# A transformer block's training step on one core: probability gradients, K heads and Q heads of the backward segments in two head halves

## The chip, the cores and the metric

The kernel runs on one core of one Trainium2 chip. The metric is the time of the whole program on the device, in microseconds (us), as a median over runs. All runs quoted here are in the same (fast) state.

Short names: PE is the tensor engine, DVE the vector engine, ACT the scalar engine, POOL GpSimd. L1129 is line 1129 of the kernel in question; the change moves lines, so that the same work has other numbers in the changed kernel (a table follows below).

## The reference, cut to what matters

A residual block: layer norm, attention with a recurrent memory of 8 rows, layer norm, SwiGLU feed-forward; then the gradients for all inputs and weights. The sequence of 2048 tokens is worked in 64 segments of 32 tokens, each with the 8 memory rows ahead of it (L = 40), 16 heads of width 256, model width 448.

```python
for s in range(n_seg):                                   # 64 segments, one after the other
    h = jnp.concatenate([mem, xs], axis=1)               # 8 memory rows + 32 tokens
    q, k, v = (einsum('btd,dhe->bhte', h, W) for W in (Wq, Wk, Wv))
    p = softmax(where(mask, einsum('bhqe,bhke->bhqk', q, k) * scale, -1e9))
    o = einsum('bhte,hed->btd', einsum('bhqk,bhke->bhqe', p, v), Wo)
    mem = o[:, :M, :]                                    # feeds the next segment
    outs.append(o[:, M:, :])
...
_out, _vjp = jax.vjp(_f, A_x, A_mem0, A_Wq, A_Wk, A_Wv, A_Wo, B_w_gate, B_w_up, B_w_down)
_grads = _vjp(grad_out)
```

The recurrence goes backwards in the gradient: the backward part walks the 64 segments from last to first, and each needs the gradient of the memory rows from the one before it. This serial walk is what the change is about.

## The kernel before

The program has four stages, one after the other: 64 forward segments, the feed-forward part, 64 backward segments, and a tail with the weight gradients. Here is one backward segment, in the kernel's order. `k.ps1()` takes a PSUM bank from a pool of five, `k.fx1()` one from a pool of two, and `k.evac` copies a bank out with DVE ("v") or ACT ("s").

```python
for s in range(NSEG - 1, -1, -1):
    t, r = divmod(s, 4)                       # r: place in the tile of 4 segments, 3 comes first
    ...
    pss = [k.ps1() for _ in range(4)]
    ...  matmul(pss[..], WoT_sb, do_roll)     # L1152 output gradients, 128 of them
    ...  evac(doT, pss[b])
    token_major(0); token_major(1)            # L1161 turned output gradients, copied by DVE / ACT
    pD = k.ps1()
    ...  matmul(pD, doT, vT)                  # L1170 probability gradients, 32
    ...  four DVE instructions pD -> dS_bd    # L1177-L1182 score gradients, all 8 head pairs at once
    heads("v", dO_sb, P_bd)                   # L1129, 16 matmuls into three banks, then copies
    rows_in("v", WvT_sb, 0, MC)               # L1201 row products, MC = 32
    heads("k", Q_sb, dS_bd)                   # L1129: needs dS_bd
    ...  turned scores, 16 small matmuls      # L1210
    rows_in("k", WkT_sb, 0, 20)
    heads("q", K_sb, dST_bd)                  # L1129: needs the turned scores
    rows_in("k", WkT_sb, 20, MC)
    rows_in("q", WqT_sb, 0, MC)
    ...
    pm = k.ps1()
    ...  matmul(pm, om, sel)                  # L1223 closing fp32 products
    ...  vector.tensor_copy(do_roll[next], pm3[:, :, 24:32])          # what the next segment needs
    nc.scalar.copy(out=dxT[:, :, r * SEG + M:(r + 1) * SEG], in_=pm3[:, :, 0:24])   # L1234
    if r == 0:                                # once per 4 segments: the block of memory rows
        px = k.fx1()
        ...  96 row products into px          # L1265: fill gaps of the NEXT segments on PE
        pl = k.fx1()
        ...  4 fp32 products into pl          # L1272 (8 instructions in the trace for the 4)
        pX = k.fx1()
        ...  4 fp32 transposes of dxT         # L1280: read the whole of dxT
        ...  layer-norm backward, store
```

First, PE works in different *forms*: the whole array (128x128), half (64 columns wide), or four strips of 32 columns; the row products run four at once, one per strip, and such a group of four is called a slot: in the trace the four start 3 to 4 ns apart, each lasts 353 ns (median), and one slot starts 0.189 us after another. Second, a scheduler orders the instructions by priority, so the 96 row products of the block of memory rows (L1265) slide into gaps of the following segments, and the fp32 work behind them (L1272, L1280) follows once they are complete.

## Time and profile before

| | us |
|---|---|
| time, median of 3 runs | 3078.84 (3069.54 to 3079.16) |
| forward stage and what lies between it and the next (profiled run) | 1030.9 |
| feed-forward stage | 301.6 |
| 64 backward segments | 1028.7 |
| tail | 713.6 |
| PE busy, whole program | 2910.6 (94%) |

The stages are read from the start times of PE's instructions in the trace: from the first query and key product of the first forward segment (L536), from the first feed-forward product (L891), from the first L1152, from the last segment's L1152 to the end. The profiled run was 3091.27.

The 64 backward segments come in four kinds, by `r`. Their periods, from one segment's first L1152 to the next one's (medians), are 16.07 us for r = 3 (15.91 in the undisturbed ones), 15.91 for r = 2, 16.79 for r = 1, 15.87 for r = 0. I call r = 3 and r = 2 the usual segments.

### The profile page before, as it was taken

How to read it: one execution, taken by the hardware profiler on the slowest of the kernel's cores; microseconds unless marked ns; L12 is line 12 of the kernel's file. 1: busy time of each engine (PE TensorE's matmuls, PEld its weight loads, DVE VectorE, ACT ScalarE, POOL GpSimd, SP SyncE). 2: the span in 40 equal slices, each digit the busy share in tenths (PEclk: the TensorE clock that was granted, in tenths of full speed). 3: DMA queues.
4: the chain of work that ended last, by engine and by line, in shares of the span. 5: the costliest groups of instructions: out<-in, count | busy, mean ns of one | idle time of the engine just before them, and what ended most of it. 6: DMA issues, size and time to landing. Idle time of an engine off the chain costs nothing.

```text
span 3089.5 us, 108321 instructions
## 1 busy us (share of the span) xinstructions
PE 2910.6 (94%) x47650; PEld 1739.2 (56%) x47650; DVE 1366.9 (44%) x3445; ACT 1054.3 (34%) x2570; POOL 676.0 (22%) x1507
## 2 busy tenths in 40 slices
PE   5999999999998999989999999999999899999999
PEld 3455555555554555556776677667776444444444
DVE  4555555555555576654545555455555001111110
ACT  2444444444444444433333333333333011111120
POOL 2222222222222222321212122212212111212111
PEclk9999999999999999989999999999999999999999
DMA  7567766766767989984455545545455998969971
GB/s 243 136 169 179 184 166 174 187 169 175 190 178 184 278 218 220 218 287 125 135 150 137 140 131 139 155 131 145 133 134 169 273 270 216 183 183 190 176 200 52
DMA packets 739468, 550.12 MB, mean 178 GB/s; under 512 B 600052, under 2 KB 635364, under 8 KB 736564
## 3 DMA queue, kind: packets, MB, share of 16 engines
q1 hardware_dynamic: 687956, 389.65, 53.0%
q0 software_dynamic: 51040, 153.54, 15.2%
q8 instruction: 374, 6.13, 0.8%
q14 instruction: 98, 0.80, 0.1%
HBM read 168.01 MB, written 234.23 MB: 130 GB/s over the span
## 4 chain that ended last, share of the span: by engine, by line
PE 68%; issue 11%; DMA 7%; DVE 7%; ACT 4%; POOL 2%; SPq 1%; ACTq 0%; POOLq 0%; DVEq 0%
PE po L1201 7%; PE psf L1152 7%; PE psf L536 6%; PE psf L653 5%; PE po L698 4%; PE psf L1376 4%; PE psf L1129 3%; PE psf L891 3%; PE fx L1015 3%; PE fx L1265 3%; PE psf L1223 2%; PE fx L465 2%; DVE arA L75 2%; PE psf L1398 2%; PE psf L550 2%
## 5 line engine op out<-in xcount | busy, mean ns | idle before, releaser
L75 DVE CAST arA<-psf 128x256 bf16<-128x256 f32 (+3 forms) x933 | 425.4, 478 | 786.2 <-PE psf L1376 275.5
L76 ACT CAST arA<-psf 128x96 bf16<-128x96 f32 (+4 forms) x915 | 353.5, 409 | 1030.7 <-PE psf L1376 261.2
L1201 PE MATMUL po<-arW,arA 128*32 128x448 bf16 x6144 | 348.1, 356 | 7.6 <-DMA arW<-Tq 3.7
L1376 PE MATMUL psf<-arW,arA 128*128 128x512 bf16 x980 | 250.2, 383 | 0.0
L1376 PEld LDWEIGHTS <-arA 128*128 128x128 bf16 x1440 | 137.1, 99 | 167.4 <-issue 19.0
L1201 PEld LDWEIGHTS <-arA 128*32 128x32 bf16 x6144 | 158.6, 97 | 126.3 <-DVE arA L75 8.4
L1152 PEld LDWEIGHTS <-arW 128*128 128x128 bf16 x8192 | 213.3, 96 | 24.3 <-issue 24.3
L1152 PE MATMUL psf<-arA,arW 128*128 128x40 bf16 x8192 | 216.7, 179 | 5.7 <-DVE arA L1227 5.1
L653 PE MATMUL psf<-arW,arA 128*64 128x512 bf16 x1536 | 216.5, 382 | 0.0
L536 PE MATMUL psf<-arW,arA 128*32 128x512 bf16 x3072 | 193.8, 385 | 12.5 <-DVE arA L739 12.5
L76 ACT COPY arA<-psf 128x512 bf16<-128x512 bf16 (+3 forms) x206 | 149.2, 725 | 120.9 <-DVE arA L75 77.3
L76 ACT CAST arB<-psf 128x64 bf16<-128x64 f32 (+3 forms) x384 | 121.9, 318 | 157.8 <-PE psf L540 106.6
L698 PE MATMUL po<-arW,arA 128*32 128x256 bf16 (+1 forms) x4096 | 141.1, 263 | 10.3 <-DVE arA L75 7.7
L75 DVE COPY arA<-psf 128x512 bf16<-128x512 bf16 (+2 forms) x204 | 104.2, 511 | 101.7 <-PE psf L550 55.8
L891 PE MATMUL psf<-arW 128*128 128x256 bf16 (+1 forms) x1288 | 146.4, 274 | 2.7 <-DVE arA L75 1.3
L891 PEld LDWEIGHTS <-arW 128*128 128x128 bf16 (+1 forms) x1344 | 102.3, 97 | 53.0 <-issue 42.1
L536 PEld LDWEIGHTS <-arA 128*32 128x32 bf16 x3072 | 70.5, 96 | 90.0 <-DVE arA L739 18.1
L1129 PEld LDWEIGHTS <-arW 128*128 128x128 bf16 x2048 | 84.4, 99 | 62.5 <-issue 53.9
L465 PE MATMUL fx<-arA,arW 128*128 128x64 bf16 (+1 forms) x2048 | 84.4, 195 | 32.6 <-ACT arB L76 19.0
L1398 PE MATMUL psf<-arW 128*128 128x448 bf16 x525 | 111.1, 352 | 0.8 <-DMA arW<-X_o 0.8
L698 PEld LDWEIGHTS <-arA 128*32 128x32 bf16 x4096 | 93.5, 96 | 32.4 <-DVE arA L75 10.9
L1438 POOL DMA_DIRECT2D out_dram<-arA x96 | 52.0, 549 | 264.3 <-DVE arA L75 260.0
(285 smaller groups left out, 4562.5 us busy)
## 6 DMA issues: line engine op xcount, KB each, us to landing
arW<-T SPq DMA_DIRECT2D x256, 128.0 KB
X_o<-arA SPq DMA_DIRECT2D x37, 512.0 KB
T<-arA SPq DMA_DIRECT2D x64, 256.0 KB
X_v<-arA POOLq DMA_DIRECT2D x32, 512.0 KB, 4.7
X_k<-arA POOLq DMA_DIRECT2D x32, 512.0 KB, 3.9
X_q<-arA POOLq DMA_DIRECT2D x32, 512.0 KB, 3.8
out_dram<-arA POOLq DMA_DIRECT2D x90, 128.0 KB, 4.3
VG<-arA SPq DMA_DIRECT2D x64, 160.0 KB
```

What stands on the lines that cost most here:

```text
L75: return nc.vector.tensor_copy(out=out, in_=in_)
L76: return nc.scalar.copy(out=out, in_=in_)
L465: nc.tensor.matmul(banks[w][:, i * 64:(i + 1) * 64], lhsT=lhsT, rhs=xr[lo:hi, kc, :], start=(kc == 0 and i == 0), stop=(kc == KC - 1), ski ...
L536: nc.tensor.matmul(banks[w][32 * q:32 * q + 32, :], lhsT=hT_roll[:, kc, sl, M:L], rhs=(Wq_sb, Wk_sb)[w][:, kc, col(q, b)], start=(kc == 0) ...
L653: nc.tensor.matmul(pV[b][64 * g:64 * g + 64, 0:512], lhsT=hT_flat[:, kc, sl * L:sl * L + 64], rhs=Wv_sb[:, kc, n * 512:(n + 1) * 512], sta ...
L698: nc.tensor.matmul(pO[32 * q:32 * q + 32, 0:w], lhsT=xblk[:, j, r * SEG:(r + 1) * SEG], rhs=Wo_sb[:, cj(j), 256 * dh:256 * dh + w], start= ...
L891: nc.tensor.matmul(ps[fp][:, f2 * 256:(f2 + 1) * 256], lhsT=Wt[lo:hi, kc, c * P:(c + 1) * P], rhs=xT[lo:hi, kc, :], start=(kc == 0 and f2 ...
L1129: nc.tensor.matmul(ps[b][:, i * 2 * L:(i + 1) * 2 * L], lhsT=lhs[:, at, :], rhs=rhs_bd[:, cl // 2, :, :].rearrange("p g n -> p (g n)"), st ...
L1152: nc.tensor.matmul(pss[b][:, jj * L:(jj + 1) * L], lhsT=WoT_sb[:, kc, c * P:(c + 1) * P], rhs=do_roll[:, kc, sl, :], start=(kc == 0), stop ...
L1201: nc.tensor.matmul(pH[32 * (j % 4):32 * (j % 4) + 32, 0:D], lhsT=blk[nm][:, j, r * SEG:(r + 1) * SEG], rhs=WT[:, cj(j), :], start=(nm == " ...
L1376: nc.tensor.matmul(pa[2 * kc + g][:, 0:w], lhsT=lhs_of(b)[:, kc * P:(kc + 1) * P], rhs=rhs_of(b, g), start=(b == 0), stop=(b == nblk - 1), ...
L1398: k.last_mm = nc.tensor.matmul(pa[i][:, 0:D], lhsT=lhs_of(b, i), rhs=rhs_of(b), start=(bi == 0), stop=(bi == m + 3))
```

## The change

The intent: K heads wait for the score gradients of all heads. If probability gradients, score gradients, K heads, turned scores and Q heads go in two halves of the heads, the first half can be under way on DVE while PE does something else, and no engine waits for the other. In the forward part, the values of heads 0 to 3 move ahead of the rest of V; in the feed-forward part, the down product takes its bank from the pool of five.

```diff
@@ forward segment
             value_rows(3)
+            values(0)
             value_rest(2, p_in)
...
-            values(0)
@@ feed-forward
-            pf = k.fx1()
+            pf = k.ps1()
@@ backward segment (cut)
-            for h in range(8):
-                ...                                  # probability gradients of all heads
-            ...                                      # score gradients, 4 DVE instructions
+            def grad_of_probs(b):
+                for h in range(4 * b, 4 * b + 4): ...
+            def grad_of_scores(b): ...               # the same 4 DVE instructions on half of the columns
+            for b in range(2):
+                grad_of_probs(b)
+                grad_of_scores(b)
...
             heads("v", dO_sb, P_bd)
-            rows_in("v", WvT_sb, 0, MC)
-            heads("k", Q_sb, dS_bd)
-            ...                                      # turned scores, all
-            rows_in("k", WkT_sb, 0, 20)
-            heads("q", K_sb, dST_bd)
-            rows_in("k", WkT_sb, 20, MC)
+            rows_in("v", WvT_sb, 0, 20)
+            half_heads("k", Q_sb, dS_bd, 0)
+            turned_scores(0)
+            rows_in("v", WvT_sb, 20, MC)
+            half_heads("k", Q_sb, dS_bd, 1)
+            turned_scores(1)
+            half_heads("q", K_sb, dST_bd, 0)
+            rows_in("k", WkT_sb, 0, 12)
+            half_heads("q", K_sb, dST_bd, 1)
+            rows_in("k", WkT_sb, 12, MC)
             rows_in("q", WqT_sb, 0, MC)
```

The line numbers of the same work:

| work | before | after |
|---|---|---|
| probability gradients | L1170 | L1173 |
| score gradients (DVE) | L1177 to L1182 | L1180 to L1185 |
| V heads | L1129 | L1129 |
| K and Q heads | L1129 | L1215 |
| row products | L1201 | L1232 |
| turned scores | L1210 | L1241 |
| closing fp32 products | L1223 | L1261 |
| ACT copy of `pm` to `dxT` | L1234 | L1272 |
| memory rows: row products, fp32 products, fp32 transposes | L1265, L1272, L1280 | L1303, L1310, L1318 |

More of the change, by code (lines that the diff above doesn't have):

```diff
@@ L1165, in backward_chain, with grad_of_scores @@
             pD = k.ps1()
-            for h in range(8):
-                for g in range(2):
-                    for dc in range(DC):
-                        j = 2 * (2 * h + dc) + g
-                        nc.tensor.matmul(pD[64 * g:64 * g + 64, h * L:(h + 1) * L], lhsT=doT[:, j, :], rhs=vT[:, 2 * h + dc, L * g:L * g + L],
-                                         start=(dc == 0), stop=(dc == DC - 1), skip_group_check=True)
+            prod_all = k.f32("f2", 8 * L, "prod")
+            def grad_of_probs(b):
+                for h in range(4 * b, 4 * b + 4):
+                    for g in range(2):
+                        for dc in range(DC):
+                            j = 2 * (2 * h + dc) + g
+                            nc.tensor.matmul(pD[64 * g:64 * g + 64, h * L:(h + 1) * L], lhsT=doT[:, j, :], rhs=vT[:, 2 * h + dc, L * g:L * g + L],
+                                             start=(dc == 0), stop=(dc == DC - 1), skip_group_check=True)
+            def grad_of_scores(b):
+                hs = slice(4 * b, 4 * b + 4)
+                pD3 = pD[:, 4 * b * L:4 * (b + 1) * L].rearrange("p (h n) -> p h n", n=L)
+                prod = prod_all[:, 4 * b * L:4 * (b + 1) * L].rearrange("p (h n) -> p h n", n=L)
+                nc.vector.scalar_tensor_tensor(out=prod, in0=pD3, scalar=k.scale, in1=P_sb[:, hs], op0=ALU.mult, op1=ALU.mult)
+                rsum = smal.tile([P, 4], FP32, name="rsum")
+                nc.vector.tensor_reduce(out=rsum[:], in_=prod, axis=AX.X, op=ALU.add)
+                nc.vector.scalar_tensor_tensor(out=prod, in0=pD3, scalar=k.scale, in1=rsum[:].unsqueeze(2).to_broadcast([P, 4, L]),
+                                               op0=ALU.mult, op1=ALU.subtract)
+                nc.vector.tensor_tensor(out=dS_bd[:, hs], in0=prod.unsqueeze(2).to_broadcast([P, 4, 2, L]), in1=P_bd[:, hs], op=ALU.mult)
+            for b in range(2):
+                grad_of_probs(b)
+                grad_of_scores(b)
             if s == 0:
@@ L1174, in backward_chain @@
                 k.tl.outs(4, 7, 0, 6)
-            pD3 = pD[:, 0:8 * L].rearrange("p (h n) -> p h n", n=L)
-            prod = k.f32("f2", 8 * L, "prod")[:].rearrange("p (h n) -> p h n", n=L)
-            nc.vector.scalar_tensor_tensor(out=prod, in0=pD3, scalar=k.scale, in1=P_sb, op0=ALU.mult, op1=ALU.mult)
-            rsum = smal.tile([P, 8], FP32, name="rsum")
-            nc.vector.tensor_reduce(out=rsum[:], in_=prod, axis=AX.X, op=ALU.add)
-            nc.vector.scalar_tensor_tensor(out=prod, in0=pD3, scalar=k.scale, in1=rsum[:].unsqueeze(2).to_broadcast([P, 8, L]),
-                                           op0=ALU.mult, op1=ALU.subtract)
-            nc.vector.tensor_tensor(out=dS_bd, in0=prod.unsqueeze(2).to_broadcast([P, 8, 2, L]), in1=P_bd, op=ALU.mult)
             pH = k.po1()
@@ L1195, in heads, with half_heads @@
                 if s == 0:
-                    k.tl.outs(*{"v": (7, 9), "k": (9, 10), "q": (10, 11)}[nm], 0, 6)
+                    k.tl.outs(*{"v": (7, 9)}[nm], 0, 6)
+            def half_heads(nm, lhs, rhs, b):
+                if b == 0:
+                    pps[nm] = [k.ps1() for _ in range(3)]
+                ps = pps[nm]
+                for cl in range(8 * b, 8 * b + 8):
+                    at = 8 * (cl // 4 % 2) + 4 * (cl // 8) + cl % 4
+                    bank, i = (b, cl % 8) if cl % 8 < 6 else (2, 2 * b + cl % 8 - 6)
+                    nc.tensor.matmul(ps[bank][:, i * 2 * L:(i + 1) * 2 * L], lhsT=lhs[:, at, :],
+                                     rhs=rhs[:, cl // 2, :, :].rearrange("p g n -> p (g n)"), start=True, stop=True)
+                for i in ((0,), (2, 1))[b]:
+                    if i < 2:
+                        v = ps[i][:, 0:12 * L].rearrange("p (j n) -> p j n", n=L)
+                        of = lambda tl, i=i: tl[:, 16 * i:16 * i + 12, :]
+                    else:
+                        v = ps[2][:, 0:8 * L].rearrange("p (e j n) -> p e j n", e=2, n=L)
+                        of = lambda tl: tl.rearrange("p (e j) n -> p e j n", j=16)[:, :, 12:16]
+                    ix = (slice(None),) * (2 if i < 2 else 3)
+                    k.evac(of(blk[nm])[ix + (slice(r * SEG, (r + 1) * SEG),)], v[ix + (slice(M, L),)], "vvs"[i])
+                    k.evac(of(lo[nm])[ix + (slice(r * M, (r + 1) * M),)], v[ix + (slice(0, M),)], "sss"[i])
+                    if s == 0 and i == 1:
+                        k.tl.outs(*{"k": (9, 10), "q": (10, 11)}[nm], 0, 6)
             def rows_in(nm, WT, j0, j1):
@@ L1204, in backward_chain, with turned_scores @@
             heads("v", dO_sb, P_bd)
-            rows_in("v", WvT_sb, 0, MC)
-            heads("k", Q_sb, dS_bd)
             pT = k.ps1()
-            for h in range(8):
-                for g in range(2):
-                    nc.tensor.matmul(pT[64 * g:64 * g + L, h * L:(h + 1) * L], lhsT=dS_bd[:, h, g, :],
-                                     rhs=ident[:, 64 * g:64 * g + L], start=True, stop=True, skip_group_check=True)
-            for g in range(2):
-                k.evac(dST_bd[64 * g:64 * g + L, :, g, :],
-                       pT[64 * g:64 * g + L, 0:8 * L].rearrange("p (h n) -> p h n", n=L), "vs"[g])
-            rows_in("k", WkT_sb, 0, 20)
-            heads("q", K_sb, dST_bd)
-            rows_in("k", WkT_sb, 20, MC)
+            def turned_scores(b):
+                for h in range(4 * b, 4 * b + 4):
+                    for g in range(2):
+                        nc.tensor.matmul(pT[64 * g:64 * g + L, h * L:(h + 1) * L], lhsT=dS_bd[:, h, g, :],
+                                         rhs=ident[:, 64 * g:64 * g + L], start=True, stop=True, skip_group_check=True)
+                for g in range(2):
+                    k.evac(dST_bd[64 * g:64 * g + L, 4 * b:4 * b + 4, g, :],
+                           pT[64 * g:64 * g + L, 4 * b * L:4 * (b + 1) * L].rearrange("p (h n) -> p h n", n=L), "vs"[g])
+            rows_in("v", WvT_sb, 0, 20)
[8 more added lines that the diff above has]
+            rows_in("k", WkT_sb, 12, MC)
             rows_in("q", WqT_sb, 0, MC)
```

## The prediction

What no trace or run of this case shows is cut out of the recorded text, and each cut is marked. The forecast's sum came to 28 - 2 - 2 = +24 us, shaded to the +19 of 3098 us. "The trace agrees" behind the first cut refers to a passage that is gone; its 0.093 us, and the 492 and 324 ns further on, are of the trace of before. *Drain* is the prediction's and the expectations' name for what a change of form adds to the distance between two starts; what PE does in that time, no trace shows. That a part-empty slot costs as much as a full one is seen in the trace after the change: a lone row product is followed by a whole-array matmul after 295 ns, one full slot after 305.

> **What bounds the kernel now.** I read the page's first part, then stretches by stage, then the waits of the tensor engine (PE) in each stage, then the timeline of one backward segment and one forward one. The page first:
>
> ```profile
> PE 2910.6 (94%) x47650; PEld 1739.2 (56%) x47650; DVE 1366.9 (44%) x3445; ACT 1054.3 (34%) x2570; POOL 676.0 (22%) x1507
> ```
>
> PE is busy nearly always; no other engine is close. By stage (columns: stretch, length, busy time of PE, PEld, DVE, ACT, POOL with counts, clock, DMA share, GB/s):
>
> ```profile
> 1034.00:1346.00 312.00, 301.25 (x2280) 183.91 (x2277) 211.06 (x340) 146.56 (x276) 91.05 (x125) 0.99 0.94 247
> 1346.00:2390.00 1044.00, 1004.98 (x23668) 726.54 (x23665) 531.36 (x1329) 371.68 (x1055) 211.22 (x482) 0.99 0.53 144
> ```
>
> The feed-forward stage (first line) leaves PE idle 10.8 us, the 64 backward segments (second line) 39.0 us, of which some 17 are at their start. The 64 forward segments lie before them, up to 1034 us; behind them comes a tail of some 700 us that the change does not touch. What PE waits for, backward, then forward, then feed-forward:
>
> ```profile
> PE psf L1129 <- DVE arB L1182: 9.4, 23, 0.4
> ```
> ```profile
> PE fx L465 <- ACT arB L76: 19.0, 40, 0.7
> PE fx L672 <- DVE arB L643: 16.7, 54, 0.6
> ```
> ```profile
> PE fx L1015 <- DVE arW L991: 7.3, 3, 3.2
> ```
>
> The wait that the head halves aim at, K heads (L1129) for score gradients (L1182), shows as 9.4 us only. This view hides part of every wait, because a matmul's modelled end is late. The timeline of PE in one backward segment (start, length, what) shows how much:
>
> ```profile
> 1802.58 0.73 PE L1129 MATMUL psf<-arB,arW 128*128 128x80 bf16 x16 [0.45 <-DVE arB L1182]
> 1803.24 0.38 PE L1210 MATMUL psf<-ident,arB 128*40 128x40 bf16 x16
> 1803.61 1.31 PE L1201 MATMUL po<-arW,arA 128*32 128x448 bf16 x21
> 1805.00 0.73 PE L1129 MATMUL psf<-arB,arW 128*128 128x80 bf16 x16
> 1805.66 2.26 PE L1201 MATMUL po<-arW,arA 128*32 128x448 bf16 x43
> 1807.57 0.73 PE L1265 MATMUL fx<-arW,arB 128*32 128x448 bf16 x9
> ```
> ```profile
> 1810.34 3.37 PE L1152 MATMUL psf<-arA,arW 128*128 128x40 bf16 x128
> 1813.55 1.12 PE L1161 MATMUL psf<-ident,arA 128*128 128x128 bf16 x16
> 1814.60 0.37 PE L1170 MATMUL psf<-arA 128*64 128x40 bf16 x12
> ```
>
> L1201 and L1265 are row products: four of them, in four strips of 32 columns, run at once, and one such slot takes 0.189 us from start to start. Note the overlaps. L1161 starts 0.16 us before the modelled end of L1152 (both in 128x128 form); L1170, in a 64-column form, starts only 0.07 before the end of L1161. The start times say the same throughout: a slot of row products is followed after 189 ns by another, after 285 ns by a full-array matmul; an 80-column head product after 36 ns by another and after 131 ns by a row product; a 128-column transpose after 56 ns by its like and after 149 by L1170. **Each change of form costs PE 0.08 to 0.10 us even when nothing is waited for.** It is no idle time in any view.
>
> [...] The trace agrees, at 0.093 us a change on average. [...] here the four of a slot start 3 to 4 ns apart, so a slot with one matmul costs as much as one with four. [...] here 128x320 fp32 from PSUM takes 492 ns (L1177) and 128x160 takes 324 (L637), so two halves cost 0.16 us more than one whole.
>
> **The change, backward.** Probability gradients (L1170), score gradients, K heads, turned scores (L1210) and Q heads go in two halves, woven into the row products. The built order of a usual segment goes from: 32 L1170, 16 V heads, 8+32+4 row products, 16 K heads, 16 turned scores, 21 rows, 16 Q heads, 54 rows; to: 16, V 8, rows 8, V 8, rows 5, 16, rows 15, K 8, turned 8, rows 15, K 8, rows 2, turned 8, Q 8, rows 8, Q 8, rows 62.
>
> Added: counted over the built orders of the whole backward part, 848 changes of form become 1398. 550 x 0.093 = 51 us. Runs of row products that do not start and end on a multiple of four leave slots part empty: 2008 slots become 2088, 80 x 0.189 = 15 us. Sum +66 us of PE time.
>
> Removed: taking each gap between PE starts above the least one of its kind (start to start, so the hidden part counts), the waits in this part sum to: rows to heads 18.8 + 3.5 us (K heads for L1182, Q heads for the turned scores' copy), the second half of the V heads for the ScalarE copy of the turned output gradient 13.1, heads and turned scores to rows 3.0 + 2.6. 41 us at most.
>
> Are they all removed? I walked one segment with the durations of the trace, time 0 being the first probability gradient. First half done at 0.42; VectorE: product to 0.78, V copy (0.55) to 1.31, sum to 1.55, difference to 1.91. In the built program the second half of the probability gradients waits for that difference, since it goes to the same bank; PE comes to it at 2.08, so it just fits. The first K half needs 2.66 and PE is there at 3.30; the second K half needs about 4.7 and PE is there at 4.74; the second Q half needs 6.42 and PE is there at 6.50. So no big new wait, but two with under 0.1 us to spare. PE then comes to the segment's closing products at 10.0 us where it took 9.73 before (median, with its waits). The two kinds of segment with the block of memory rows differ more (about +1.4 for one, 0 for the other). Walk: 16 x (0.3 + 0.3 + 1.4 + 0) = +32; count: 66 - 41 = +25. I take **+28 us**.
>
> **Forward.** The values of heads 0 to 3 move ahead of the last quarter of V. This kills the two waits shown above; start to start they are 19.0 (L672) and 21.7 + 8.0 us (after L672). But VectorE now copies the first values between the reciprocal and the last product of the softmax, so the probabilities come 0.33 us later, and three output rows that the built order puts ahead of L672 wait about 0.45 us for that copy, in some 60 segments: 27 us back. Changes of form 1480 to 1597: 11 us. Part-empty slots 53 x 0.112 = 6 us. Sum 27 + 11 + 6 - 49 = -5. Walking one segment gives the closing transpose at +0.0 to +0.1 us in the 49 or so segments with filler (L465), where 5 of these now split the output rows, and -0.36 us in the dozen without: near -1. I take **-2 us**.
>
> **Feed-forward.** The down product leaves the pool of two banks for that of five, so the following product no longer needs L991 to empty one. It still needs L997, which ends 0.54 us before L991 in the one I looked at; three such waits: 3 x 0.54 = **-2 us**, not 7.
>
> Sum: 28 - 2 - 2 = +24 us on 3078.84.
>
> **Rivals.** (1) The waits are the real cost and the drains are hidden: then backward gains 41, forward up to 20, together -50 to -60 us, 3025. For it: the change plainly follows the waits. Against it: 285 against 189 ns appears at the least gap too, where nothing is waited for. (2) The bank shared by both halves becomes the bound: the second half of the probability gradients waits for VectorE, and everything behind it by 0.3 to 0.5 us, so none of the 41 us are won and the total is +66 or more, 3140. For it: the slack is 0.17 us in my walk, and in segments with layer-norm work VectorE has 2 us more to do. Against it: VectorE is 51% busy in this stage. (3) Later loads: the load of the V rows, which can only start after the second half, starts 2 us later. In the trace PE waited for it once, 0.4 us, so I expect nothing.
>
> **Range and chances.** Rounding the sum down a little for rival 1, which I cannot exclude in part: 3098 us, range 3066 to 3130. The runs of before alone spread over 10 us. Over 2% either way needs -61 or +62 us: the first more than all waits that I found, the second all drains and no wait gone. Chances 0.02 faster, 0.91 same, 0.07 slower.
>
> **What would show it.** The backward stretch at about 1070 us with PE's busy time up (modelled ends pile up at more drains) and idle time down; the wait for L1182's successor near zero; usual segments of 16.2 us where they were 15.9; start gaps of 285 and 131 ns at the new changes. Forward within 5 us, with a new wait of the output rows for the VectorE copy. The wait for L991 gone, replaced by L997 at nearly the same time. I am wrong if backward segments get shorter than 15.8 us, if a wait of the second half of the probability gradients shows in most segments, or if forward segments change by over 0.2 us.

## The result, and the profile after

The changed kernel takes 3118.17 us (median of 4 runs, 3114.22 to 3118.94), against 3079.0 (3069.54 to 3082.9) for the kernel before in the same rounds. The ratio is 1.0129, with a 95% interval of 1.0105 to 1.0154. A ratio here is the mean time of one kernel's fast runs over that of the other's of the same rounds, so it isn't quite the ratio of the medians quoted. The change loses 39 us where 19 were forecast: slower, clear of the noise, though inside the range given, and twice the forecast loss.

The page's first line, for comparison with the one in the prediction:

```profile
PE 2991.1 (96%) x47650; PEld 1749.4 (56%) x47650; DVE 1410.9 (45%) x3637; ACT 1086.0 (35%) x2762; POOL 676.5 (22%) x1507
```

PE has the same 47650 matmuls and is busy 80 us longer, which is not 80 us of more work: a busy span ends at a matmul's modelled end, and the spans now overlap less (in before a transpose L1161 starts 0.15 us ahead of the modelled end of the L1152 before it, in the same form, and L1170, in another form, only 0.07 ahead of that of L1161; medians). DVE has 192 instructions more, three for each segment. Two halves cost it more than a whole: the first score-gradient instruction took 492 ns at 128x320 (L1177 of before) and takes 325 at 128x160 (L1180; medians), two thirds of the time for half the columns. The stretches by stage say where (columns as in the prediction: stretch, length, busy time of PE, PEld, DVE, ACT and POOL with their counts, clock, DMA share, GB/s; feed-forward first, then backward):

```profile
1030.00:1341.00 311.00, 302.64 (x2293) 185.23 (x2291) 212.09 (x345) 147.44 (x277) 91.72 (x125) 0.99 0.94 250
1341.00:2414.00 1073.00, 1048.60 (x23298) 720.19 (x23294) 567.56 (x1488) 395.18 (x1221) 204.33 (x471) 0.99 0.49 137
```

The stretch of before in the prediction (1346 to 2390) isn't cut alike: it runs on some 14 us into the last segment. Its forecast of "about 1070 us" is that cut of 1044 us and 28 more, so the 1073.00 here is no hit. From the first L1152 of the first segment to that of the last the stage is 1028.7 us against 1073.0, **+44.3 us**. The other stages of the profiled run are no longer than before: forward 1027.2, feed-forward 299.8, tail 702.3. So the whole loss lies in the 64 backward segments. In stretches cut alike at the stage's ends (1347.2 to 2375.9 and 1341.5 to 2414.5), PE is busy 1048.6 us against 990.5, +58.1, and idles 24.4 against 38.2, -13.8. The wait that the halves aimed at is gone. What PE waits for in the backward stretch (waiting engine, its tile and line, releaser, us in total, times, longest):

```profile
PE psf L1129 <- ACT arA L76: 7.9, 17, 0.5
...
PE po L1232 <- DVE arA L75: 2.6, 14, 0.2
```

and the line of that wait in before:

```profile
PE psf L1129 <- ACT arA L76: 0.4, 1, 0.4
```

Nothing is left of the score gradients (9.4 us before, at L1182), but a wait has come up that the kernel before hardly had: 17 times about 0.5 us, V heads (L1129) for ACT. There are 16 tiles of four segments; this is once per tile. In the forward stretch:

```profile
PE po L698 <- DVE arA L75: 11.4, 49, 0.3
...
PE fx L672 <- DVE arB L643: 1.4, 5, 0.6
```

The old wait at L672 (16.7 us) has nearly gone, that of L465 (19.0) altogether, and the output rows (L698) wait for the VectorE copy instead, as forecast. In the feed-forward stretch, L991 is replaced by L997, as forecast too:

```profile
PE psf L891 <- ACT arA L76: 4.5, 1, 4.5
PE fx L1015 <- DVE arA L997: 1.5, 1, 1.5
```

The first line is a wait that the forecast didn't have: once 4.5 us for ACT, where before waited once 1.3 us for VectorE at L891.

By kind of segment (median period of before, of after, the sum over the stage's segments of that kind):

| kind | before, us | after, us | change of the sum, us | per segment | forecast |
|---|---|---|---|---|---|
| r = 3 | 16.07 | 16.31 | 267.5 to 272.6 = +5.1 | +0.3 | +0.3 |
| r = 2 | 15.91 | 16.31 | 255.8 to 262.3 = +6.5 | +0.4 | +0.3 |
| r = 1 | 16.79 | 16.62 | 267.4 to 266.0 = -1.4 | -0.1 | 0 |
| r = 0 | 15.87 | 18.21 | 238.0 to 272.1 = +34.1 | **+2.3** | +1.4 |

(The last segment has no successor, so the sum for r = 0 is over 15.) More than three quarters of the loss lie in one segment of four. First a usual one, r = 3; PE's timeline, start, length and what:

```profile
1829.26 0.43 PE L1173 MATMUL psf<-arA 128*64 128x40 bf16 x16
1829.62 0.46 PE L1129 MATMUL psf<-arB,arA 128*128 128x80 bf16 x8
1830.01 0.56 PE L1303 MATMUL fx<-arW,arB 128*32 128x448 bf16 x8
1830.51 0.46 PE L1129 MATMUL psf<-arB,arA 128*128 128x80 bf16 x8
1830.90 0.55 PE L1232 MATMUL po<-arW,arA 128*32 128x448 bf16 x5
1831.38 0.43 PE L1173 MATMUL psf<-arA 128*64 128x40 bf16 x16
...
1834.47 0.36 PE L1232 MATMUL po<-arW,arA 128*32 128x448 bf16 x2
1834.77 0.27 PE L1241 MATMUL psf<-ident,arB 128*40 128x40 bf16 x8
1834.97 0.46 PE L1215 MATMUL psf<-arB,arW 128*128 128x80 bf16 x8
```

No line carries a wait, yet each line is in another form than the one above it. Two row products (L1232 at 1834.47) hold PE for 0.30 us until L1241 starts: a slot of 0.189 and the change of form. Then the fourth kind, r = 0, at the same place:

```profile
1811.17 0.53 PE L1310 MATMUL fx<-sel,om 128*128 128x32 f32 x3
...
1811.60 0.41 PE L1173 MATMUL psf<-arA 128*64 128x40 bf16 x14
1812.49 0.39 PE L1129 MATMUL psf<-arB,arA 128*128 128x80 bf16 x6 [0.49 <-ACT arA L76]
1812.72 0.63 PE L1318 MATMUL fx<-identf,arB 128*128 128x128 f32 x4
1813.53 0.36 PE L1232 MATMUL po<-arW,arA 128*32 128x448 bf16 x1 [0.18 <-DVE arA L75]
1813.83 0.28 PE L1129 MATMUL psf<-arB,arA 128*128 128x80 bf16 x3
```

Half of the fp32 products of the memory rows (L1310) and all their transposes (L1318) now lie in this segment. In before all of them ran in the one ahead of it, r = 1:

```profile
1786.72 1.06 PE L1272 MATMUL fx<-sel,om 128*128 128x32 f32 x8
...
1792.33 0.66 PE L1280 MATMUL fx<-identf,arB 128*128 128x128 f32 x4
```

and the V heads of r = 0 had nothing to wait for:

```profile
1799.32 1.01 PE L1129 MATMUL psf<-arB,arA 128*128 128x80 bf16 x16
```

How far they slid can be read from the timelines: by segment, from r = 0 on through the next tile's r = 3 and r = 2 to its r = 1, before takes in 21, 32, 32 and 11 of the 96 memory-row products, after 21, 28, 28 and 19; so the 96 are complete later. (Why a usual segment takes four fewer, the traces don't tell; one gap fewer to fill is a guess.) And there is a second thing: in r = 0 V heads go in pieces of 6, 3 and 7, where the usual segment has 8 and 8. Here is ACT in the same stretch:

```profile
1811.43 1.01 ACT L76 COPY arA<-psf 128x1024 bf16<-128x1024 bf16 x1 [0.75 <-PE psf L1161]
...
1813.38 0.52 ACT L1272 COPY arB<-psf 128x96 f32<-128x96 f32 x3 [0.73 <-PE fx L1318]
```

At 1813.38 ACT makes *three* copies L1272 in a row, released by the transposes L1318: those of r = 3, r = 2 and r = 1. Until then each of the three `pm` held one of the five banks, so two were left. The first V heads had to wait until ACT had emptied the bank with the turned output gradients (the copy that starts at 1811.43 and takes 1.01 us; they start at 1812.49, 0.05 us after its end); the next ones have a semaphore of ACT ahead of them, which the copies L1272 counted up at 1813.63, 1813.77 and 1813.92 (which count they wait for, the trace doesn't tell), and start at 1813.83. That is 0.295 us after the row product ahead of them, the distance at which V heads start after a lone row product in all 29 such places of the stage (295 to 296 ns), so nothing shows that the copies held back these. What the held banks cost, experiment 5 tests.

### The profile page after: what moved, and what is told of

Its sections match the earlier page's. It is cut to its first block, busy times and chain, and to the rows that moved or that the text cites. A ratio compares the mean times of both kernels' runs of the same rounds, so it can differ in the third digit from the quotient of the medians.

```text
span 3116.9 us, 108765 instructions
## 1 busy us (share of the span) xinstructions
PE 2991.1 (96%) x47650; PEld 1749.4 (56%) x47650; DVE 1410.9 (45%) x3637; ACT 1086.0 (35%) x2762; POOL 676.5 (22%) x1507
## 4 chain that ended last, share of the span: by engine, by line
PE 70%; issue 13%; DMA 4%; DVE 3%; ACT 3%; POOL 2%; SPq 1%; POOLq 0%; ACTq 0%; DVEq 0%
PE po L1232 11%; PE psf L1152 7%; PE psf L536 5%; PE po L698 4%; PE psf L653 4%; PE psf L891 4%; PE psf L1414 4%; PE psf L1215 3%; PE fx L1303 3%; PE fx L1015 2%; PE psf L1261 2%; PE psf L550 2%; PE psf L1161 2%; PE psf L1129 2%; PE psf L540 1%
## 5 line engine op out<-in xcount | busy, mean ns | idle before, releaser
L75 DVE CAST arA<-psf 128x384 bf16<-128x384 f32 (+5 forms) x869 | 446.1, 516 | 747.2 <-PE psf L1414 275.2
L76 ACT CAST arA<-psf 128x256 bf16<-128x256 f32 (+6 forms) x979 | 363.2, 385 | 1018.4 <-PE psf L1414 261.2
L1232 PE MATMUL po<-arW,arA 128*32 128x448 bf16 x6144 | 402.6, 357 | 7.9 <-DMA arW<-Tq 2.9
L1152 PEld LDWEIGHTS <-arW 128*128 128x128 bf16 x8192 | 213.5, 96 | 17.9 <-issue 17.9
L1152 PE MATMUL psf<-arA,arW 128*128 128x40 bf16 x8192 | 217.8, 180 | 0.8 <-DVE arA L1265 0.8
L1232 PEld LDWEIGHTS <-arA 128*32 128x32 bf16 x6144 | 150.9, 96 | 116.3 <-ACT arA L76 10.1
L76 ACT CAST arB<-psf 128x64 bf16<-128x64 f32 (+3 forms) x512 | 146.3, 286 | 198.1 <-PE psf L540 109.7
L698 PE MATMUL po<-arW,arA 128*32 128x256 bf16 (+1 forms) x4096 | 165.6, 263 | 13.8 <-DVE arA L75 11.4
L75 DVE COPY arA<-psf 128x512 bf16<-128x512 bf16 (+2 forms) x204 | 104.3, 512 | 114.9 <-PE psf L550 55.7
L891 PE MATMUL psf<-arW 128*128 128x256 bf16 (+1 forms) x1288 | 149.0, 276 | 6.1 <-ACT arA L76 4.5
L891 PEld LDWEIGHTS <-arW 128*128 128x128 bf16 (+1 forms) x1344 | 103.4, 97 | 58.0 <-issue 46.4
L1215 PEld LDWEIGHTS <-arW 128*128 128x128 bf16 x2048 | 85.0, 100 | 72.7 <-issue 60.5
L698 PEld LDWEIGHTS <-arA 128*32 128x32 bf16 x4096 | 99.8, 96 | 45.6 <-DVE arA L75 29.5
L1083 POOL DMA_DIRECT2D arB<-P_all x64 | 35.0, 546 | 383.4 <-DVE arA L75 278.6
L1215 PE MATMUL psf<-arB,arW 128*128 128x80 bf16 x2048 | 117.8, 203 | 0.1
```

What stands on the lines that cost most here:

```text
L75: return nc.vector.tensor_copy(out=out, in_=in_)
L76: return nc.scalar.copy(out=out, in_=in_)
L698: nc.tensor.matmul(pO[32 * q:32 * q + 32, 0:w], lhsT=xblk[:, j, r * SEG:(r + 1) * SEG], rhs=Wo_sb[:, cj(j), 256 * dh:256 * dh + w], start= ...
L891: nc.tensor.matmul(ps[fp][:, f2 * 256:(f2 + 1) * 256], lhsT=Wt[lo:hi, kc, c * P:(c + 1) * P], rhs=xT[lo:hi, kc, :], start=(kc == 0 and f2 ...
L1152: nc.tensor.matmul(pss[b][:, jj * L:(jj + 1) * L], lhsT=WoT_sb[:, kc, c * P:(c + 1) * P], rhs=do_roll[:, kc, sl, :], start=(kc == 0), stop ...
L1215: nc.tensor.matmul(ps[bank][:, i * 2 * L:(i + 1) * 2 * L], lhsT=lhs[:, at, :], rhs=rhs[:, cl // 2, :, :].rearrange("p g n -> p (g n)"), st ...
```

## The experiments

The theory: backward loses by changes of form (time of PE at each) more than it wins by waits removed, and in the fourth kind three held banks add a new wait. The rivals: that time is hidden and something else makes the segments longer (rival 1 of the prediction); the bank that both halves of the probability gradients share is the bound (rival 2); the forward part takes a share. All twelve kernels gave correct results. "Before" beside a time is the kernel before in the same rounds on the same chip.

### 1 and 2: the parts alone

The first kernel has the forward and feed-forward lines of the change only, the second the backward lines only.

```diff
 e1: before, with
+            values(0)          # ahead of value_rest(2, p_in)
-            pf = k.fx1()
+            pf = k.ps1()
 e2: after, without these three lines
```

> The forward and feed-forward parts of the change alone, the backward segments as before. By stage the changed kernel's profile has -3.3 us forward, -0.3 between, -1.8 us feed-forward, so about -5 us, 3074 us, ratio 0.998. If the loss of 39 us comes from outside the backward segments (a rival: the moved values delay the softmax), this run is slower than before, by 10 us or more.

> The backward part alone. Theory (form changes, part-empty slots of row products and held PSUM banks in the backward segments): the whole loss and the 5 us that the rest wins, +44 us, 3123 us, ratio 1.0144. Rival (parts disturb each other): less than +35.

Measured: 3083.74 us for the first (before 3081.64; ratio 0.9982, 0.9946 to 1.0019), 3119.82 for the second (ratio 1.0101, 1.0058 to 1.0145). The backward stage took 1027.6 us in the first and 1073.2 in the second, against 1028.7 before and 1073.0 after. So the loss is that of the backward lines, and the stage repeats within about 1 us. The total doesn't repeat as well: the second kernel lost some 31 us by the ratio and 38 by the medians where 44 were expected, before alone ran from 3074 to 3106 us in these rounds, and the tail, which no kernel here changes, took 702 to 726 us in the profiled runs. From here on the stage and the segment periods are the measure, and the totals only the check.

### 3 and 4: changes of form alone

Before, with four tiny matmuls (8 columns of output, into columns of the bank that nobody reads) put among the last row products of each segment; once in the form of the whole array, once in that of a strip. The first adds changes of form, the second adds the same instructions without them.

```diff
-            rows_in("q", WqT_sb, 0, MC)
+            for j0 in range(0, MC, 8):
+                rows_in("q", WqT_sb, j0, j0 + 8)
+                nc.tensor.matmul(pH[0:128, D:D + 8], lhsT=ident[:, 0:128], rhs=ident[:, 0:8], start=False, stop=False, ...)
 (e4: 32 in place of 128)
```

> The kernel before with four tiny matmuls a segment, of 8 columns into unused columns of the row products' bank, in 128x128 form among the closing row products: 476 more changes of form over the backward part (850 to 1326, counted in the built order) and nothing to wait for. Theory of drains: 0.095 us a change, so +45 us over the same dummies in 128x32 form. Rival (drains are hidden and the loss is all new waits): within 10 us of it.

> The same four tiny matmuls a segment in the 128x32 form of the row products: no change of form added (850). Both theories: 256 matmuls of some 25 ns in one of four strips, 0 to +7 us over before.

Measured: 3134.31 (ratio 1.0163, 1.0112 to 1.0214) with the whole-array form, 3083.27 (ratio 0.9989, 0.9945 to 1.0033) with the strip form; backward 1082.8 and 1031.1. PE's timeline with the whole-array form, one dummy (L1220) to the next, then with the strip form:

```profile
1839.36 0.18 PE L1220 MATMUL po<-ident 128*128 128x8 bf16 x1
1839.47 0.56 PE L1201 MATMUL po<-arW,arA 128*32 128x448 bf16 x8
1839.96 0.18 PE L1220 MATMUL po<-ident 128*128 128x8 bf16 x1
```

```profile
1811.06 0.17 PE L1220 MATMUL po<-ident 128*32 128x8 bf16 x1
1811.08 0.70 PE L1201 MATMUL po<-arW,arA 128*32 128x448 bf16 x8
1811.46 0.17 PE L1220 MATMUL po<-ident 128*32 128x8 bf16 x1
```

Eight row products and a dummy repeat every 0.60 us in the first and every 0.40 in the second: 0.10 us per change of form, with nothing that could be waited for. It is paid each way: eight row products to the dummy take 0.49 us and the dummy to the next row product 0.11, where two slots alone take 0.38. The tiny matmul in the form already in use costs 0.02 to 0.03 us (0.02 at 1811.06, 0.40 us less two slots; its expectation had some 25 ns, which is the distance between starts of the 40-column products L1152 in before). Over the stage, 850 changes became 1326, and 1082.8 - 1031.1 = 51.7 us over 476 is 0.109 each; why it is a little more than in the timeline, no run tells. The prediction's 0.093, taken from gaps between starts, holds, and rival 1 falls: the cost of a change of form is not hidden. No line of the timeline carries a wait in brackets: it shows only in the distance from one start to the next. In the busy time of PE over the stage it hides as work: 1047.1 us with the whole-array dummies, 992.0 with those of strip form, at the same number of matmuls.

### 5: the three banks set free

After, with the ACT copy going to a small tile of its own, so that `pm` gives its bank back at once; GpSimd takes the columns on to `dxT` when that is free. (The tile is bf16, so these columns are rounded; the result is still within tolerance.)

```diff
+    pm_st = [...]                                   # three small tiles, one for each r > 0
-            nc.scalar.copy(out=dxT[:, :, r * SEG + M:(r + 1) * SEG], in_=pm3[:, :, 0:24])
+            if r > 0: nc.scalar.copy(out=pm_st[3 - r], in_=pm3[:, :, 0:24])      # (one in two parts)
+            else:     nc.scalar.copy(out=dxT[...], in_=pm3[:, :, 0:24])
+        if r > 0:     nc.gpsimd.tensor_copy(out=dxT[...], in_=pm_st[3 - r])
```

> The changed kernel, but the 96 columns that each segment leaves for the input gradient go at once to a small bf16 tile and from there by GpSimd to their place, so that their PSUM bank is not held until the transposes of the block of memory rows are done. Changes of form are as in the changed kernel (1400 to 1396), row slots 2109 to 2094. Theory (in the fourth kind of segment, which takes 18.2 us against 15.9 before, the V heads wait for banks held by three segments): that kind falls by 0.5 us or more and the total by 8 to 20 us, to about 3104. Rival (the fourth kind is slow because the fp32 products were moved into it, which is only a shift): within 4 us of the changed kernel.

Measured: 3102.84 (before 3088.73; ratio 1.0041, 1.0012 to 1.0070). Backward took 1049.5 us, 23.5 less than after, at 1396 changes of form and 2094 slots, nearly the 1400 and 2109 of after. (The counts recorded with the experiments differ a little from the prediction's, 848 to 1398 and 2008 to 2088; by them before has 850 and 2029, so the differences are the same.) By kinds 16.31, 16.31, 16.18, 16.98: the usual ones are untouched, r = 1 is 0.44 shorter and r = 0 is 1.23 shorter. The fourth kind in this kernel (V heads are L1130, the fp32 products L1324):

```profile
1798.62 0.43 PE L1174 MATMUL psf<-arA 128*64 128x40 bf16 x16
1798.99 0.46 PE L1130 MATMUL psf<-arB,arA 128*128 128x80 bf16 x8
1799.28 1.06 PE L1324 MATMUL fx<-sel,om 128*128 128x32 f32 x8
1800.28 0.46 PE L1130 MATMUL psf<-arB,arA 128*128 128x80 bf16 x8
```

V heads go in 8 and 8 again, and PE's wait for ACT there fell from 7.9 us to 1.4 in the stage:

```profile
PE psf L1130 <- ACT arA L76: 1.4, 3, 0.6
```

So setting the banks free takes 23.5 us off the backward stage of after, more than was expected. Not all of it is waiting: the scheduler also made another order (the eight fp32 products, for one, now nearly always run together in r = 0), and what each of the two brings was not parted by a run. By start times (see the account below) some 16 us of it are waits.

### 6: a bank for each half

After, with the second half of the probability gradients in a bank of its own, so that it needn't wait until DVE has read the first (rival 2).

```diff
-            pD = k.ps1()
+            pDs = [k.ps1(), k.ps1()]
             def grad_of_probs(b):
+                pD = pDs[b]
             def grad_of_scores(b):
+                pD = pDs[b]
```

> The changed kernel, but each half of the probability gradients has its own PSUM bank, so the second half need not wait for VectorE to have read the first. The scheduler then makes another order: 1400 changes of form become 1102, row slots 2109 become 2011. Theory of drains and slots: 298 x 0.093 + 98 x 0.189 = 46 us less than the changed kernel, less whatever waits come back: 3072 to 3100. Rival (the waits rule, and the shared bank is the wait): a gain too, but without fewer gaps of 285 and 131 ns; PE's waits in the backward part fall instead.

Measured: 3138.46 (before 3088.73; ratio 1.0169, 1.0139 to 1.0199), no faster than after (1.0105 to 1.0154), with *fewer* changes of form (1102) and slots (2011). A miss: 46 us less were expected. The backward stage took 1083.0 us, 10.0 more than after, but the granted clock was lower, 0.983 to 0.985 in all four runs against 0.991 and 0.992. In 11 of the 16 segments r = 1 the output gradients went slower; both of these lines are of this kernel, the first at the usual speed (r = 2), the second slower (r = 1):

```profile
1841.67 3.37 PE L1152 MATMUL psf<-arA,arW 128*128 128x40 bf16 x128
...
1859.82 4.21 PE L1152 MATMUL psf<-arA,arW 128*128 128x40 bf16 x128
```

Over the stage the starts within L1152 lie 8.5 us further apart than in after (214.8 against 206.3), so most of the 10.0 us lies there. The clock granted in the stage was 0.97 against 0.99 in after; whether it is the cause of the 8.5 us, and why it is lower, no run tells. By kinds 16.59, 18.15, 17.26, 16.36; the fp32 products lie in r = 2 now. DVE shows where a wait came from. Its timeline in this kernel (L1182 is the first score-gradient instruction of a half, L1187 the last, L75 with 128x384 the copy of the first V heads):

```profile
1813.49 0.33 DVE L1182 SCALAR_TENSOR_TENSOR prod<-psf,arB 128x160 f32<-128x160 f32 x1 [0.23 <-PE psf L1174]
...
1814.08 0.31 DVE L1182 SCALAR_TENSOR_TENSOR prod<-psf,arB 128x160 f32<-128x160 f32 x1
...
1814.77 0.48 DVE L1187 TENSOR_TENSOR arB<-prod,arB 128x320 bf16<-128x320 f32 x1
...
1815.40 0.55 DVE L75 CAST arA<-psf 128x384 bf16<-128x384 f32 x1
```

and the same in the usual segment of after (L1180 and L1185 are those instructions):

```profile
1829.74 0.32 DVE L1180 SCALAR_TENSOR_TENSOR prod<-psf,arB 128x160 f32<-128x160 f32 x1 [0.20 <-PE psf L1173]
1830.05 0.56 DVE L75 CAST arA<-psf 128x384 bf16<-128x384 f32 x1
...
1831.44 0.48 DVE L1185 TENSOR_TENSOR arB<-prod,arB 128x320 bf16<-128x320 f32 x1
```

Where both halves are there at once, DVE starts on both, and finishes the first, before it copies V heads; the V rows then have no input, the built order goes to the K heads instead, and PE waits there for the score gradients:

```profile
PE psf L1217 <- DVE arB L1187: 17.8, 32, 0.7
```

In after, the shared bank keeps the second half back, and DVE copies V heads 0.3 us after the first score instruction (1.9 here). And in after the second half doesn't wait for its bank: from the five row products at 1830.90 (two slots and a change of form) it follows at 1831.38, with no idle time. So the shared bank isn't the bound, and rival 2 falls. That it is of use as a brake is not parted from the rest of this experiment, which also has one bank fewer for others and another order.

### 7 and 8: the two kinds of halves apart

The first has the gradients whole and the heads in halves, the second the gradients in halves and the heads whole; both with the new forward and feed-forward lines.

```diff
 e7: after, with grad_of_probs / grad_of_scores of all 8 head pairs in one go, as in before
 e8: before (forward and feed-forward lines changed), with
+            for b in range(2):
+                grad_of_probs(b)
+                grad_of_scores(b)
```

> The changed kernel with the probability and score gradients whole again, only K heads, turned scores and Q heads in halves: 1166 changes of form, 2044 row slots (before: 850 and 2029). Theory: + 316 x 0.093 + 15 x 0.189 = +32 us on before, less at most 5 us of the wait of Q heads that it removes, less 5 us of the forward part: about 3100. Rival (halves of the heads are what helps, halves of the gradients what hurts): at or under 3074.

> The probability and score gradients in halves, the heads whole as before, forward and feed-forward parts changed: 1053 changes of form, 2093 row slots. Theory: + 203 x 0.093 + 64 x 0.189 = +31 us on before, less some 15 us of the V heads' wait that the new order fills, less 5 us of the forward part: about 3090. Rival (as above): at or over the changed kernel's 3118.

Measured: 3152.66 (before 3088.73; ratio 1.0215, 1.0186 to 1.0245) with heads in halves, 3108.07 (ratio 1.0063, 1.0028 to 1.0099) with gradients in halves. The first is a miss: 64 us over before of the same rounds, where some 21 were expected; its usual segments took 16.57, +0.67, and r = 1 took 18.71. The second came nearer (19 us over before, some 11 expected): usual segments 15.96, so halving the gradients alone costs only 0.05 us there, but r = 1 took 17.43 and r = 0 took 17.13. In both, the excess over the usual segments sits where the fp32 work of the memory rows lies, so each was run again with the tile of experiment 5.

### 9 to 12: the same with the banks set free

```diff
 e9:  forward and feed-forward lines + the tile of experiment 5; backward order as before
 e10: e8 + the tile
 e11: e6 + the tile
 e12: e7 + the tile
```

> Forward and feed-forward parts changed, backward segments as before but with the small bf16 tile that frees the banks early (790 changes of form, 2014 row slots). Theory (held banks cost the kernel before, too, in the third kind of segment, 16.8 us against 15.9): that kind falls to 15.9 to 16.1, the others stay; with 5 us from the other parts 15 to 20 us under before, ratio 0.994: faster than both kernels. Rival (the third kind is longer because of the fp32 products in it): ratio 0.998 as in the run without the tile.

> Gradients in halves, heads whole, with the small tile: 1038 changes of form. Without held banks all four kinds of segment should lie near the 15.96 us that the first two took with the banks held; backward about 1028 us, 10 us over the kernel with whole gradients and the tile. Rival (held banks are not what lengthens the third and fourth kinds): those stay at 17.4 and 17.1.

> Each half of the probability gradients in its own bank, with the small tile: 997 changes of form. By the count of changes alone it should beat the changed kernel with the tile (1396) by 37 us and more with its slots; but in the run without the tile the K heads waited 0.7 to 1.1 us for V copies, one bank fewer being free. So theory of banks: no better than it, kinds one and four at 16.3 to 16.6, kinds two and three down from 18.1 and 17.3 to 16.6 to 17. Rival (count of changes alone): backward under 1020 us.

> Heads in halves, gradients whole, with the small tile: 1031 changes of form. The first two kinds stay at 16.57 us, the third falls from 18.7 to about 16.6: backward about 1060 us, 40 us over whole heads with the tile. If the third kind stays over 17.5, the held banks are not its cause.

Measured (before 3081.12): e9 3084.66 (ratio 0.9994, 0.9957 to 1.0030), e10 3076.64 (0.9993, 0.9939 to 1.0047), e11 3127.34 (1.0136, 1.0093 to 1.0179), e12 3116.41 (1.0114, 1.0064 to 1.0164). Put together, the length of the backward stage in each profiled run:

| backward order | `pm` holds its bank, us | bank set free, us | difference |
|---|---|---|---|
| as before | 1028.7 | 1024.6 (e9) | 4.1 |
| gradients in halves | 1057.9 (e8) | 1023.1 (e10) | 34.8 |
| heads in halves | 1097.5 (e7) | 1065.2 (e12) | 32.3 |
| both (after) | 1073.0 | 1049.5 (e5) | 23.5 |
| both, own bank for each half | 1083.0 (e6) | 1075.2 (e11) | 7.8 |

The right column is what setting the banks free brings, new order included: 4 and 8 us in two of the orders, 23 to 35 in the other three. The middle column is the change without this: halved gradients cost nothing (-1.5 us against e9), halved heads cost +40.6, both together +24.9. So halved gradients *help* once the heads are in halves, by 15.7 us, presumably because the first K half then finds its scores ready (in e12 PE waited 7.3 us for them, in e5 not at all; it also waited 8.0 us for a load, T0k, in e5 0.8); but the halved heads pay for themselves in none of these orders.

The number of changes of form alone doesn't order these kernels: e11 has 997 and takes 1075.2 us, e5 has 1396 and takes 1049.5 (of these 26 us some 12 lie in the output gradients, whose starts are 219.2 us apart in sum against 206.9, at a clock of 0.982 against 0.991). Waits count as well; the order on DVE that experiment 6 showed is the one here too (PE waited 19.3 us for L1188, the same instruction). Its r = 2 and r = 1 took 17.35 and 17.25, where 16.6 to 17 was expected. (That expectation has K heads wait 0.7 to 1.1 us for V copies in e6; the view of waits there has them wait for the score gradients, L1187, 0.7 us at most.) In e10 three kinds lie at or under the 15.96 expected, but r = 0 took 16.63.

A hoped-for gain was missed: e9 was to be clearly faster than before. Its r = 1 segments did fall from 16.79 to 16.30, but the stage won only 4.1 us, and the total is not to be told from that of before. e10 has the shortest backward stage of all, 5.6 us below before, and its total ties with before as well. No version here clearly beats the kernel before.

## Why the prediction was right or wrong

**What bounds the kernel: right.** PE, and within it spacing between starts rather than idle time. Its busy time rose by 58 us in the backward stage without one more matmul.

**Changes of form cost time by themselves: right.** 0.093 us was read from gaps; 0.10 to 0.11 was measured with dummies that nothing waits for (e3 against e4). Rival 1, a gain of 50 to 60 us, falls with it.

**Waits removed: half right.** The wait for the score gradients went to nothing, and the second half of the probability gradients doesn't wait for its bank, as the walk had it. Start to start, as the prediction counted, the kinds of gap of which it summed 41 us hold 41.7 us in before and 3.9 in after, so nearly all of them went. But new ones came that no step of the prediction had, 18 us in all: 7.9 between the probability gradients and V heads, 3.6 ahead of the row product behind the fp32 transposes, 2.4 ahead of turned scores, and 4.1 more among the transposes that turn the output gradient. In e5 the first three are nearly nil and the last is 1.9.

**The step that failed: the size of "The two kinds of segment with the block of memory rows differ more (about +1.4 for one, 0 for the other)".** It measured +2.3 for r = 0 and -0.1 for r = 1: +34.1 us and -1.4 over the stage, where 16 x 1.4 = 22 were allowed. These 12 us are nearly the whole miss of the walk, 44.3 against 32. The walk followed the data from one instruction to the next, and took these two kinds from the built order. It did not follow who holds a PSUM bank. With the fp32 transposes of the memory rows slid from r = 1 into r = 0, three `pm` hold banks until they have run, and V heads stall (17 times, 7.9 us). This step, not the waits or the changes of form of the usual segments, is the one that was wrong. By medians r = 0 rose by 2.34 us and r = 1 fell by 0.17, together +2.17; with the banks set free (e5) they would be +1.11 and -0.61, together +0.50. The other 1.67 us of each tile go when the banks are set free.

**The count of changes of form and slots less all waits, +25: its terms right, the new waits missing.** e5 against e9, both with free banks, is 1049.5 - 1024.6 = +24.9. That this is the forecast's number to a tenth is luck, for the forecast's counts were those of another pair. But on the counts of these two (790 to 1396 changes, 2014 to 2094 slots, 47 us of waits of the same kinds in e9) the rule gives 56 + 15 - 47 = +24, so it holds where no bank is held. Setting the banks free brings 23.5 us in after and 4.1 in before; the difference, 19.4, is by the way it is formed the rest of the 44.3. A check that isn't formed so: 51 + 15 for changes of form and slots, less 38 us of waits that went, and 18 that came, is +46 against +44.3. I then went from a sum of +24 down to +19 "for rival 1"; that shading was a step away from what was measured. How much of the rise of r = 0 that e5 keeps is fp32 work moved there, and how much changes of form, was read from the orders and not isolated by a run.

**Usual segments, +0.3: nearly right.** +0.3 and +0.4 (15.91 to 16.31 in most, so +0.4). From the halves of the heads alone it would be +0.67; the halved gradients give some back.

**Forward, -2: right as far as it can be seen.** The two waits went and the output rows' wait for the copy came, as described. Ten kernels with the new lines have a forward stage of 1028.2 us on average, four with the old lines 1029.9: -1.7, single stages scattering by 1.5.

**Feed-forward, -2: not resolved.** The wait changed hands as described and the one at L891 came, and the same two groups average 297.1 and 297.0 us, with single values from 294 to 302. No gain is shown.

**Rival 2, the shared bank: rightly held unlikely.** Giving each half its own bank gained nothing: the stage became longer (e6 1083.0 us against 1073.0, e11 1075.2 against 1049.5), at a lower granted clock (0.983 and 0.982 against 0.991).

The sum: backward +44.3 where +28 was taken; forward and feed-forward together near -2 where -4 was taken; so some +42 where +24 was the sum and +19 was put down. The measured +39 has an interval of 32 to 47 us (1.0105 and 1.0154 less 1, times 3079), which holds it.

## What to carry to other kernels

Count the changes of PE's form before interleaving: here each costs 0.1 us that no idle time and no wait shows, and a split that turns 13 of them in a segment into 22 must remove waits of 0.9 us to break even. When work slides later, ask which buffers it keeps occupied: a single buffer read late can hold several PSUM banks of another stage, and a small tile to copy into at once can free them: here it took 23.5 us off the backward stage of after and 4.1 off that of before. Judge such changes by the period of the repeating segment, kind by kind, not by a total in which an untouched tail scatters by 20 us.
